# Weight gradients of a SwiGLU FFN: seven Strassen block products in place of eight for four of the five row tiles of dw_gate and dw_up

## The chip, the core and the metric

The kernel runs on one core of one Trainium2 chip. The core has a matrix engine (TensorE, PE in the profile; its weight loads are listed apart as PEld), three engines for elementwise work (VectorE: DVE; ScalarE: ACT; GpSimd: POOL) and SyncE (SP), which here only issues DMAs. Each engine executes its own instructions in order. DMAs are issued from the queues of SP, ACT and POOL and move data between HBM (DRAM), the on-chip memory SBUF and back, some of them transposing on the way. TensorE writes its results to PSUM, which the other engines read. The metric is the device time of one execution in microseconds, and the number compared is the median of several runs.

## The reference

The kernel computes the forward pass and all gradients of a linear-attention block followed by a SwiGLU FFN, in bfloat16, with S = 2048 rows, D = 640 and F = 1728:

```python
def _B_ref(x, w_gate, w_up, w_down):
    g = _silu(x @ w_gate)
    u = x @ w_up
    return (g * u) @ w_down
...
h = x + _A_ref(_layernorm(x, axis=-1), A_wqkv, A_wo)
h2 = h + _B_ref(_layernorm(h, axis=-1), B_w_gate, B_w_up, B_w_down)
...
_out, _vjp = jax.vjp(_f, A_x, A_wqkv, A_wo, B_w_gate, B_w_up, B_w_down)
_grads = _vjp(grad_out)
```

The change is in the gradients of the FFN's weights. With `hn` the normalised `h` (2048 x 640), `m` the product of silu(gate) and up (2048 x 1728), `dh2` the incoming gradient (2048 x 640), and `dg`, `du` the gradients at the outputs of the gate and the up projection (2048 x 1728 each), they are

    dw_gate = hn^T dg      (640 x 1728, out_4)
    dw_up   = hn^T du      (640 x 1728, out_5)
    dw_down = m^T dh2      (1728 x 640, out_6; first computed transposed, as dh2^T m)

## The kernel before

Rows are cut into 16 tiles of 128 (`ST`), the 640 columns of `hn` and `dh2` into 5 tiles of 128 (`DT`). The attention block comes first (up to L607); its last loop writes `h1` (tiles of the pool `work`, stored to DRAM as `scr_h1`) and forms `hn` and its transpose `hnT`. The FFN part (L611 to L731) goes through F in four groups of columns, `GW` = 448, 448, 448 and 384 wide. A group g has two stages:

- **The loop** over eight pairs of row tiles (t = 0, 2, ..., 14). Ten matmuls fill `pg` (L639) and ten `pu` (L644), both halves of one PSUM tile; in group 2 ten more fill `pdm`, while groups 0, 1 and 3 find that product (`dm`) made earlier. ScalarE forms sigmoid(pg) into `dd` (L660), sigmoid(-pg) into `nsg` (L664), and copies `pg` to `m_s` (L665) and `pu` to `u` (L666). VectorE makes `m_s` (m), and in `dd` the `dg` and `du`, by seven elementwise operations (L672). For each row tile SP issues a DMA that transposes its 2w values of `dd` into a `stg` tile (L675, three buffers), and GpSimd issues its store to `scr_dT` (L676). Every second pair GpSimd also stores four row tiles of `m_s` to `scr_m` (L678).
- **The gradient stage.** `dw()` (L702) takes up to two products ("parts"), each a sum over the 16 row tiles, so 16 matmuls into one half of a PSUM tile `ps_dw` (L711). Then one copy takes the tile to a `dwev` tile (L713), and GpSimd issues a store for each part (L715). A `dwd_part(i)` is tile i of dw_down transposed (`dh2` against `m_s`, stored to `scr_dwdT`), a `dgu_part(i, which)` is tile i of dw_gate or dw_up (`hn` against the gate or up half of `dd`, stored to out_4 or out_5). The order is dwd 0 and 1, dgu 0, dgu 1, dwd 2 and 3, dgu 2, dgu 3, dwd 4, dgu 4; dw_down's copies are on VectorE, the others on ScalarE. In all 15 parts, 240 matmuls. The first `dw` puts the row tiles 14 and 15 last (`first=True`), since the loop's elementwise work ends on them.

PSUM is one pool of four tiles of 2 x 512 float32 per partition, taken in turn by `mm(name)`. SBUF is in pools too: `fpool` has six buffers of 2 x 448 bfloat16 per partition that `nsg`, `u`, `a` and `dwev` take in turn (`fw`), and it lies in the area `wB`, opened when the attention block's area `fA` (the tile `rr`) is closed at L609. `work`, with six buffers of 640, is open from start to end; `wk()` takes tiles from it in the attention block and, in the stage after the FFN, in `ln_bwd` (L142), the backward of the layer norm.

`hn` stands as [128, 16, 640]: partition, row tile, column. `dd` is two tiles of eight row tiles each, [128, 8, 896], the gate half and the up half side by side. `m_s` is [128, 16, 448].

The framework's scheduler may reorder an engine's instructions within the limits of their dependencies; in this block (L616) `manual_schedule` fixes SyncE's order as written, and the other engines are left to the scheduler. Waits between engines are put in by the framework from the tiles' uses: a PSUM tile is tracked as a whole, a pool's buffer is handed out again when its last user is done, and so is the area of a closed pool.

After the FFN's last group comes the stage of `ps_dhn` (L109), which takes the transposed `dd` back from `scr_dT` as `cols` tiles. `load_cols(0)` is issued on ScalarE's queue at the start of group 3's gradient stage, `load_cols(1)` in it, behind dwd 4.

Of the kernel before, what the change touches and what calls it, by code (L numbers as in the profile page):

```python
# [20 lines left out]
def kernel(  # L21
# [36 lines left out]
    big = ctx.enter_context(tc.tile_pool(name="big", bufs=5))  # L58
    strips = ctx.enter_context(tc.tile_pool(name="strips", bufs=4))
    small = ctx.enter_context(tc.tile_pool(name="small", bufs=4))  # L60
    work = ctx.enter_context(tc.tile_pool(name="work", bufs=6))

    def mm(name):

# [5 lines left out]
    def half(ap):  # L70
        return ap.rearrange("p (c n) -> p c n", c=2)

    wpools = [work]

    def wk(name, w=D, pool=0):
        return wpools[pool].tile([P, w], BF16, name=name, tag="w", padded_shape=[P, D])
# [98 lines left out]

    fA = ExitStack()
    rr = fA.enter_context(tc.tile_pool(name="fA", bufs=1)).tile([P, 4, 2, D], BF16, name="rr")

    def fw(name):
        return fpool.tile([P, 2, GM], BF16, name=name, tag="f")  # L180
# [430 lines left out]
    fpool = wB.enter_context(tc.tile_pool(name="fpool", bufs=6))  # L611
    zpad = wB.enter_context(tc.tile_pool(name="zpool", bufs=1)).tile([P, 4, 64], BF16, name="zpad")
    nc.gpsimd.memset(zpad[:], 0.0)

    with tc.manual_schedule(engines={EngineType.SP}):
        dh2 = big.tile([P, ST, D], BF16, name="dh2", tag="B")  # L616

        def load_dh2():
# [11 lines left out]
        for g in range(4):  # L630
# [71 lines left out]
            def dw(parts, copy, first=False):  # L702

                ps = mm("ps_dw")
                steps = [(c, t) for c in range(len(parts)) for t in range(ST)]
                if first:

                    steps.sort(key=lambda x: x[1] >= ST - 2)
                for c, t in steps:
                    lhs, rhs, _ = parts[c]  # L710
                    nc.tensor.matmul(ps[:, c, :w], lhsT=lhs(t), rhs=rhs(t), start=(t == 0), stop=(t == ST - 1))  # L711
                ev = fw("dwev")
                last = copy(out=ev[:, :len(parts), :w], in_=ps[:, :len(parts), :w])  # L713
                for c, (_, _, dst) in enumerate(parts):
                    nc.gpsimd.dma_start(out=dst[:, GO[g]:GO[g] + w], in_=ev[:, c, :w])  # L715
                return last
# [6 lines left out]
                        lambda t: dd[t // 8][:, t % 8, which * w:(which + 1) * w],  # L723
                        (out_4, out_5)[which][i * P:(i + 1) * P])

            for i in range(DT):
                if i % 2 == 0:
                    dw([dwd_part(k) for k in range(i, min(i + 2, DT))], nc.vector.tensor_copy, first=(i == 0))
                    if g == 3 and i == 4:
                        load_cols(1, act_load)  # L730
                dw([dgu_part(i, 0), dgu_part(i, 1)], nc.scalar.copy)  # L731

    wB.close()

    M = ctx.enter_context(tc.tile_pool(name="M", bufs=1))
    wpools.append(ctx.enter_context(tc.tile_pool(name="workC", bufs=7)))

    mats = M.tile([P, 3 * DT * D], BF16, name="mats", tag="M")
# [361 lines left out]
```

## Time and the profile before

Three runs took 815.38, 810.91 and 811.22 us: median 811.22. The profiled execution has a span of 809.9 us from the first to the last instruction, 1.3 us under that median, which also takes in what lies around it. The granted TensorE clock is full in every slice.

The stages of the FFN part, from the profile's sums over windows of time (us; the last stage of each group is the gradient stage):

| stage | from | to | length | PE busy | DVE busy | ACT busy | POOL busy |
|---|---|---|---|---|---|---|---|
| all before the FFN | 0 | 141.0 | 141.0 | 139.5 | 123.4 | 73.9 | 49.0 |
| group 0, loop | 141.0 | 172.3 | 31.3 | 31.3 | 28.9 | 25.7 | 10.2 |
| group 0, gradients | 172.3 | 217.7 | 45.4 | 45.4 | 8.4 | 5.3 | 15.7 |
| group 1, loop | 217.7 | 248.1 | 30.4 | 30.4 | 25.5 | 26.0 | 6.6 |
| group 1, gradients | 248.1 | 293.6 | 45.5 | 45.5 | 8.2 | 5.2 | 13.0 |
| group 2, loop (with `pdm`) | 293.6 | 339.0 | 45.4 | 45.4 | 35.8 | 27.6 | 9.8 |
| group 2, gradients | 339.0 | 384.4 | 45.4 | 45.4 | 6.6 | 3.6 | 9.9 |
| group 3, loop | 384.4 | 410.2 | 25.8 | 25.8 | 21.7 | 22.7 | 5.8 |
| group 3, gradients | 410.2 | 449.2 | 39.0 | 39.0 | 7.8 | 4.7 | 18.1 |
| all after the FFN | 449.2 | 809.9 | 360.7 | 357.9 | 207.0 | 90.8 | 68.6 |

How to read it: busy times are sums of the instructions' own spans on an engine; the shape of an instruction is given as partitions x elements with its type, out before in. A row of the groups names line, engine, operation, tiles and count, then busy time and the mean of one in ns, and after the second bar how long the engine was idle just before such instructions and what ended that. In the timeline a row is start, length, engine, line and tiles, and in brackets the wait before it. The DMA table gives, for each kind of transfer, the median from its issue to its landing: `scr_dT` stores from GpSimd's queue 3.2 us at 224 KB and 2.9 at 192 KB, `out_dram` stores from `dwev` 2.1 at 112 KB, `scr_m` stores 4.4 at 448 KB, and `cols` loads on ScalarE's queue 9.8 at 1728 KB.

### The profile page before, as it was taken

To read this page: it belongs to the slowest core of one execution; us is meant where nothing else is said; L and a number is where in the kernel's file an instruction comes from. 1 tells how busy PE (TensorE), PEld (TensorE's weight loads), DVE (VectorE), ACT (ScalarE), POOL (GpSimd) and SP (SyncE) were. 2 spreads that over 40 slices of the span, in tenths; PEclk is the share of its full clock that TensorE was granted. 3 is DMA by queue.
4 is the path that set the end of the run, shared out by engine and by line. 5 is a ranking of instruction groups with operands and counts; after the bars stand their busy time and mean duration, and the time that the engine had idled before them with its cause. 6 is when DMAs were issued, how large, how long until landed. Compare 5 with 4: busy or idle time off the path is not lost.

```text
span 809.9 us, 13757 instructions
## 1 busy us (share of the span) xinstructions
PE 805.5 (99%) x5421; PEld 516.9 (64%) x5421; DVE 473.2 (58%) x883; ACT 285.4 (35%) x398; POOL 206.8 (26%) x369
## 2 busy tenths in 40 slices
PE   9999999999999999999999999999999999999998
PEld 7676566555555555555656677777777777777676
DVE  7989988880095028810850148999897366631212
ACT  6963532750283035400831122322323133322010
POOL 4600047322422312221226301211221121112330
PEclk9999999999999999999999999999999999999999
DMA  9899999997679978991597757977499988999993
GB/s 255 164 246 312 181 244 265 233 259 178 190 168 206 198 189 192 215 252 54 119 242 179 244 149 213 226 195 174 115 208 168 175 154 168 169 239 210 245 214 101
DMA packets 281584, 160.11 MB, mean 198 GB/s; under 512 B 241564, under 2 KB 267293, under 8 KB 281520
## 3 DMA queue, kind: packets, MB, share of 16 engines
q1 hardware_dynamic: 259696, 85.40, 57.8%
q0 software_dynamic: 18928, 68.52, 26.6%
q10 hardware_dynamic: 2896, 5.33, 2.1%
q8 instruction: 42, 0.69, 0.4%
q14 instruction: 22, 0.18, 0.1%
HBM read 47.68 MB, written 53.66 MB: 125 GB/s over the span
## 4 chain that ended last, share of the span: by engine, by line
PE 98%; DVE 1%; DMA 1%; POOL 0%; issue 0%; DVEq 0%
PE ps_dw L711 22%; PE ps_dhn L109 14%; PE ps_dxn L971 8%; PE ps_o L1029 7%; PE pu L644 7%; PE pg L639 7%; PE ps_dwqk L894 5%; PE ps_dm L417 5%; PE ps_kq L305 4%; PE ps_dp L109 3%; PE ps_gt L769 3%; PE ps_y L508 3%; PE ps_dk L109 3%; PE ps_a L571 3%; PE pdm L417 2%; DMA xnT<-xn 1%
## 5 line engine op out<-in xcount | busy, mean ns | idle before, releaser
L109 PE MATMUL ps_dhn<-wgT,cols 128*128 128x320 bf16 x864 | 119.5, 299 | 0.0
L711 PE MATMUL ps_dw<-dd,hn 128*128 128x448 bf16 (+1 forms) x640 | 118.8, 346 | 0.0
L109 PEld LDWEIGHTS <-cols 128*128 128x128 bf16 x864 | 84.4, 98 | 33.0
L711 PEld LDWEIGHTS <-hn 128*128 128x128 bf16 x640 | 62.5, 98 | 54.3
L713 DVE CAST dwev<-ps_dw 128x896 bf16<-128x896 f32 (+3 forms) x12 | 10.9, 907 | 124.6 <-PE ps_dw L711 109.5
L676 POOL DMA_DIRECT2D scr_dT<-stg x64 | 34.7, 542 | 166.2 <-DMA stg<-dd 162.4
L713 ACT CAST dwev<-ps_dw 128x896 bf16<-128x896 f32 (+1 forms) x20 | 17.6, 878 | 160.2 <-PE ps_dw L711 150.8
L147 DVE CUSTOM_DVE_ANT_0 lb_a<-lb_dy,hn 128x640 bf16<-128x640 bf16 x32 | 26.4, 826 | 64.4 <-ACT lb_dy L145 64.4
L644 PE MATMUL pu<-wgu,hnT 128*128 128x448 bf16 (+1 forms) x320 | 63.6, 346 | 0.0
L639 PE MATMUL pg<-wgu,hnT 128*128 128x448 bf16 (+1 forms) x320 | 63.6, 346 | 0.0
L1029 PE MATMUL ps_o<-wd,mT 128*128 128x320 bf16 (+3 forms) x462 | 61.1, 296 | 0.0
L711 PE MATMUL ps_dw<-m_s,dh 128*128 128x448 bf16 (+1 forms) x320 | 60.4, 346 | 0.0
L971 PEld LDWEIGHTS <-ring 128*128 128x128 bf16 x480 | 46.9, 98 | 18.3
L1029 PEld LDWEIGHTS <-mT 128*128 128x128 bf16 (+1 forms) x462 | 41.7, 97 | 17.5 <-issue 2.6
L971 PE MATMUL ps_dxn<-wqkvT,ring 128*128 128x320 bf16 x320 | 51.3, 299 | 0.0
L711 PEld LDWEIGHTS <-dh 128*128 128x128 bf16 x320 | 31.3, 98 | 27.1
L644 PEld LDWEIGHTS <-hnT 128*128 128x128 bf16 x320 | 31.3, 98 | 27.1
L639 PEld LDWEIGHTS <-hnT 128*128 128x128 bf16 x320 | 31.3, 98 | 27.1
L417 PEld LDWEIGHTS <-dh2T 128*128 128x128 bf16 x320 | 31.0, 98 | 25.1
L417 PE MATMUL ps_dm<-wdT,dh2T 128*128 128x448 bf16 (+1 forms) x240 | 46.5, 344 | 0.0
L305 PE MATMUL ps_kq<-wqk,xnT 128*128 128x320 bf16 x320 | 45.0, 300 | 0.4 <-DMA xnT<-xn 0.4
L145 ACT ACTIVATE lb_dy<-ps_dhn,rstd 128x640 bf16<-128x640 f32 x16 | 12.7, 793 | 86.2 <-PE ps_dhn L109 86.2
(168 smaller groups left out, 1306.7 us busy)
## 6 DMA issues: line engine op xcount, KB each, us to landing
scr_dT<-stg POOLq DMA_DIRECT2D x48, 224.0 KB, 3.2
cols<-scr_dT POOLq DMA_DIRECT2D x6, 1728.0 KB, 8.4
scr_m<-m_s POOLq DMA_DIRECT2D x12, 448.0 KB, 4.4
cols<-scr_dT ACTq DMA_DIRECT2D x2, 1728.0 KB, 9.8
out_dram<-dwev POOLq DMA_DIRECT2D x30, 112.0 KB, 2.1
scr_dT<-stg POOLq DMA_DIRECT2D x16, 192.0 KB, 2.9
scr_pq<-pqa SPq DMA_DIRECT2D x4, 640.0 KB, 4.7
scr_xnT<-xnT SPq DMA_DIRECT2D x4, 640.0 KB, 5.3
```

The source lines that it names most:

```text
L109: nc.tensor.matmul(ps[:, ci, :320], lhsT=lhs(k), rhs=rhs(k, *NCH[ci]), start=(start and k == 0), stop=(stop and k == n - 1))
L147: nc.vector.tensor_tensor_reduce(out=a[:], in0=dy[:], in1=xhat, scale=1.0, scalar=0.0, op0=ALU.mult, op1=ALU.add, accum_out=sums[:, 1:2])
L305: nc.tensor.matmul(ps[:, ci, :320], lhsT=xnT[:, t, k, :], rhs=wqk[:, k, w0 + n0:w0 + n1], start=(k == 0), stop=(k == DT - 1))
L417: nc.tensor.matmul(ps[:, c, :w], lhsT=dh2T[:, kt, (t + c) * P:(t + c + 1) * P], rhs=wdT[:, kt, o:o + w], start=(kt == 0), stop=(kt == DT - 1))
L639: nc.tensor.matmul(pg[:, c, :w], lhsT=hnT[:, kt, (t + c) * P:(t + c + 1) * P], rhs=wg[:, kt, 0:w], start=(kt == 0), stop=(kt == DT - 1))
L644: nc.tensor.matmul(pu[:, c, :w], lhsT=hnT[:, kt, (t + c) * P:(t + c + 1) * P], rhs=wg[:, kt, w:2 * w], start=(kt == 0), stop=(kt == DT - 1))
L676: nc.gpsimd.dma_start(out=scr_dT[t + c, :, KO[g]:KO[g] + GK[g], :], in_=stg[:, :GK[g], :])
L711: nc.tensor.matmul(ps[:, c, :w], lhsT=lhs(t), rhs=rhs(t), start=(t == 0), stop=(t == ST - 1))
L713: last = copy(out=ev[:, :len(parts), :w], in_=ps[:, :len(parts), :w])
L894: nc.tensor.matmul(ps[:, ci, :320], lhsT=xn_r[:, t, i * P:(i + 1) * P], rhs=dq[t // 8][:, t % 8, n0:n1] if which == 0 else dk[:, t, n0:n1] ...
L971: nc.tensor.matmul(ps[:, ci, :320], lhsT=lhs[:, i, :], rhs=rhs[:, i, n0:n1], start=(k == 0 and i == 0), stop=(k == 2 and i == DT - 1))
L1029: nc.tensor.matmul(po(t, ci), lhsT=mTs[t // 4][r, t % 4, j, :], rhs=wd[r, j, n0:n1], start=(t, ci) not in opened, stop=last)
```

## The change

For the first four column tiles of `hn`, the two products (gate and up) are computed by Strassen's scheme in Winograd's form, with seven block products in place of eight. `A` stands for the transposed `hn` in 2 x 2 blocks, `B` for `dd` in 2 x 2 blocks: A_mk has the column tiles 2m and 2m+1 and the row tiles of half k (8 of 16), B_kn the row tiles of half k of gate (n = 1) or up (n = 2). Then

    S1 = A21 + A22,  S2 = S1 - A11,  S3 = A11 - A21,  S4 = A12 - S2
    T1 = B12 - B11,  T2 = B22 - T1,  T3 = B22 - B12,  T4 = B21 - T2
    U1 = A11 B11 + A12 B21 = C11            (gate, column tiles 0 and 1)
    U2 = A11 B11 + S2 T2
    U3 = U2 + S3 T3
    C21 = U3 + A22 T4                       (gate, column tiles 2 and 3)
    C22 = U3 + S1 T1                        (up, column tiles 2 and 3)
    C12 = U2 + S1 T1 + S4 B22               (up, column tiles 0 and 1)

Each block product is made for two column tiles (u = 0, 1), each of them 8 matmuls (`prod`, `more`): 7 x 2 x 8 = 112 matmuls where the four column tiles took 4 x 2 x 16 = 128 before. Column tile 4 is done by `dw()` as before, and so is dw_down. A stage has 224 matmuls.

What goes with it:

- The sums S1 to S4 are made on VectorE from `hn`, 8 x 128 = 1024 elements a partition at a time, into tiles of a new pool `sums`; T1, T2 and T3 on VectorE in place of blocks of `dd[0]` and T4 into `m_s`, 8 x 448 (group 3: 8 x 384) elements a partition each.
- Three PSUM tiles are held through the stage: `ps_wa` accumulates A11 B11, then S2 T2, S3 T3 and A22 T4 on top; `ps_wd` takes A12 B21; `ps_wc` S1 T1 and, on top, S4 B22.
- `keep` copies a partial result out of `ps_wa` on ScalarE, in float32, into a `part` tile, which takes one buffer of `fpool`: six in a stage. `evac` adds a kept partial to what stands in PSUM on VectorE and writes the result to `dwev` (C21: a plain copy on ScalarE), a column tile at a time; its stores are on GpSimd's queue as before.
- The order in the stage is written out, and `manual_schedule` now takes in TensorE, VectorE and ScalarE in the FFN's block beside SyncE.
- `load_cols(1)` is issued at the end of group 3's stage.
- `work` is no longer open from start to end: its six buffers lie in `fA` up to the FFN (`workA`), and a new pool `work` is opened when `wB` is closed.

In the built program two things differ outside the gradient stages: the operation that makes `a` stands before the first `nsg` on VectorE in the loops, and the memset of `zpad` stands behind the stores of `h1` on GpSimd.

```diff
@@ -58,7 +58,6 @@
     big = ctx.enter_context(tc.tile_pool(name="big", bufs=5))
     strips = ctx.enter_context(tc.tile_pool(name="strips", bufs=4))
     small = ctx.enter_context(tc.tile_pool(name="small", bufs=4))
-    work = ctx.enter_context(tc.tile_pool(name="work", bufs=6))
 
     def mm(name):
 
@@ -70,7 +69,7 @@
     def half(ap):
         return ap.rearrange("p (c n) -> p c n", c=2)
 
-    wpools = [work]
+    wpools = []
 
     def wk(name, w=D, pool=0):
         return wpools[pool].tile([P, w], BF16, name=name, tag="w", padded_shape=[P, D])
@@ -175,6 +174,7 @@
 
     fA = ExitStack()
     rr = fA.enter_context(tc.tile_pool(name="fA", bufs=1)).tile([P, 4, 2, D], BF16, name="rr")
+    wpools.append(fA.enter_context(tc.tile_pool(name="workA", bufs=6)))
 
     def fw(name):
         return fpool.tile([P, 2, GM], BF16, name=name, tag="f")
@@ -611,8 +611,9 @@
     fpool = wB.enter_context(tc.tile_pool(name="fpool", bufs=6))
     zpad = wB.enter_context(tc.tile_pool(name="zpool", bufs=1)).tile([P, 4, 64], BF16, name="zpad")
     nc.gpsimd.memset(zpad[:], 0.0)
-
-    with tc.manual_schedule(engines={EngineType.SP}):
+    sums = wB.enter_context(tc.tile_pool(name="sums", bufs=1))
+
+    with tc.manual_schedule(engines={EngineType.SP, EngineType.PE, EngineType.DVE, EngineType.Activation}):
         dh2 = big.tile([P, ST, D], BF16, name="dh2", tag="B")
 
         def load_dh2():
@@ -723,16 +724,111 @@
                         lambda t: dd[t // 8][:, t % 8, which * w:(which + 1) * w],
                         (out_4, out_5)[which][i * P:(i + 1) * P])
 
-            for i in range(DT):
-                if i % 2 == 0:
-                    dw([dwd_part(k) for k in range(i, min(i + 2, DT))], nc.vector.tensor_copy, first=(i == 0))
-                    if g == 3 and i == 4:
-                        load_cols(1, act_load)
-                dw([dgu_part(i, 0), dgu_part(i, 1)], nc.scalar.copy)
+            V, A = nc.vector, nc.scalar
+            B11, B12 = dd[0][:, :, 0:w], dd[0][:, :, w:2 * w]
+            B21, B22 = dd[1][:, :, 0:w], dd[1][:, :, w:2 * w]
+
+            def hn_blk(m, k, u):
+                i = 2 * m + u
+                return hn[:, 8 * k:8 * k + 8, i * P:(i + 1) * P]
+
+            def sub(out, in0, in1, op=ALU.subtract):
+                V.tensor_tensor(out=out, in0=in0, in1=in1, op=op)
+
+            def hn_sum(n, u):
+
+                S[n, u] = sums.tile([P, 8, P], BF16, name=f"S{n}", tag=f"S{n}")
+                in0, in1, op = {1: (lambda: hn_blk(1, 0, u), lambda: hn_blk(1, 1, u), ALU.add),
+                                2: (lambda: S[1, u][:], lambda: hn_blk(0, 0, u), ALU.subtract),
+                                3: (lambda: hn_blk(0, 0, u), lambda: hn_blk(1, 0, u), ALU.subtract),
+                                4: (lambda: hn_blk(0, 1, u), lambda: S[2, u][:], ALU.subtract)}[n]
+                sub(S[n, u][:], in0(), in1(), op)
+
+            def prod(ps, u, lhs, rhs, start, stop):
+                for t in range(8):
+                    nc.tensor.matmul(ps[:, u, :w], lhsT=lhs[:, t, :], rhs=rhs[:, t, :],
+                                     start=(start and t == 0), stop=(t == 7), skip_group_check=not start)
+
+            def part32():
+                return fw("part").rearrange("p c n -> p (c n)").bitcast(FP32)[:, :w]
+
+            def out_w(n, m, ev, u0, nu):
+                for u in range(u0, u0 + nu):
+                    i = 2 * m + u
+                    nc.gpsimd.dma_start(out=(out_4, out_5)[n][i * P:(i + 1) * P, GO[g]:GO[g] + w], in_=ev[:, u, :w])
+
+            S, s1, u2, u3 = {}, {}, {}, {}
+            ev = {}
+
+            def evac(n, m, u, in0, in1=None):
+                if (n, m) not in ev:
+                    ev[n, m] = fw("dwev")
+                if in1 is None:
+                    A.copy(out=ev[n, m][:, u, :w], in_=in0)
+                else:
+                    sub(ev[n, m][:, u, :w], in0, in1, ALU.add)
+                out_w(n, m, ev[n, m], u, 1)
+
+            def keep(d, u, ps):
+                d[u] = part32()
+                A.copy(out=d[u], in_=ps[:, u, :w])
+
+            dw([dwd_part(0), dwd_part(1)], V.tensor_copy, first=True)
+            hn_sum(1, 0)
+            dw([dgu_part(4, 0), dgu_part(4, 1)], A.copy)
+            hn_sum(2, 0)
+            hn_sum(3, 0)
+            hn_sum(4, 0)
+            pa, pd, pc = mm("ps_wa"), mm("ps_wd"), mm("ps_wc")
+            for u in range(2):
+                prod(pa, u, hn_blk(0, 0, u), B11, True, False)
+                keep(s1, u, pa)
+            sub(B11, B12, B11)
+            prod(pd, 0, hn_blk(0, 1, 0), B21, True, True)
+            evac(0, 0, 0, pd[:, 0, :w], s1[0])
+            dw([dwd_part(4)], V.tensor_copy)
+            prod(pc, 0, S[1, 0], B11, True, False)
+            hn_sum(1, 1)
+            prod(pd, 1, hn_blk(0, 1, 1), B21, True, True)
+            evac(0, 0, 1, pd[:, 1, :w], s1[1])
+            prod(pc, 1, S[1, 1], B11, True, False)
+            sub(B12, B22, B12)
+            sub(B11, B22, B11)
+            dw([dwd_part(2), dwd_part(3)], V.tensor_copy)
+            T4 = m_s[:, 0:8, :w]
+
+            def more(u, lhs, rhs, last=False):
+                prod(pa, u, lhs, rhs, False, last)
+
+            more(0, S[2, 0], B11)
+            keep(u2, 0, pa)
+            sub(T4, B21, B11)
+            hn_sum(2, 1)
+            more(1, S[2, 1], B11)
+            keep(u2, 1, pa)
+            more(0, S[3, 0], B12)
+            keep(u3, 0, pa)
+            hn_sum(3, 1)
+            evac(1, 1, 0, pc[:, 0, :w], u3[0])
+            more(1, S[3, 1], B12)
+            keep(u3, 1, pa)
+            evac(1, 1, 1, pc[:, 1, :w], u3[1])
+            more(0, hn_blk(1, 1, 0), T4, True)
+            evac(0, 1, 0, pa[:, 0, :w])
+            prod(pc, 0, S[4, 0], B22, False, True)
+            hn_sum(4, 1)
+            evac(1, 0, 0, pc[:, 0, :w], u2[0])
+            more(1, hn_blk(1, 1, 1), T4, True)
+            evac(0, 1, 1, pa[:, 1, :w])
+            prod(pc, 1, S[4, 1], B22, False, True)
+            evac(1, 0, 1, pc[:, 1, :w], u2[1])
+            if g == 3:
+                load_cols(1, act_load)
 
     wB.close()
 
     M = ctx.enter_context(tc.tile_pool(name="M", bufs=1))
+    wpools[0] = ctx.enter_context(tc.tile_pool(name="work", bufs=6))
     wpools.append(ctx.enter_context(tc.tile_pool(name="workC", bufs=7)))
 
     mats = M.tile([P, 3 * DT * D], BF16, name="mats", tag="M")
```

## The prediction

> **What bounds the kernel now.** First the page's busy shares and its chain of waits, for the engine that sets the end:
>
> ```profile
> PE 805.5 (99%) x5421; PEld 516.9 (64%) x5421; DVE 473.2 (58%) x883; ACT 285.4 (35%) x398; POOL 206.8 (26%) x369
> ...
> PE 98%; DVE 1%; DMA 1%; POOL 0%; issue 0%; DVEq 0%
> ```
>
> TensorE runs without a gap, so a matmul taken away is worth its full pace, and a wait put before a matmul costs its full length. The pace stands in the chain in order of time (start, length):
>
> ```profile
> 172.50 45.40 PE ps_dw L711 x240
> ...
> 410.36 39.00 PE ps_dw L711 x240
> ```
>
> 45.40/240 = 0.189 us per 448-column matmul, 39.00/240 = 0.1625 in group 3. Then the rows, by shape, of what the new work resembles:
>
> ```profile
> L672 DVE TENSOR_TENSOR m_s<-m_s,u 128x896 bf16<-128x896 bf16 x24 | 14.8, 619 | 0.0
> ...
> L713 ACT CAST dwev<-ps_dw 128x896 bf16<-128x896 f32 x15 | 13.6, 905 | 123.3 <-PE ps_dw L711 123.3
> ...
> L672 DVE TENSOR_TENSOR m_s<-m_s,u 128x768 bf16<-128x768 bf16 x8 | 4.4, 553 | 0.0
> ...
> L713 ACT CAST dwev<-ps_dw 128x768 bf16<-128x768 f32 x5 | 4.0, 799 | 36.9 <-PE ps_dw L711 27.5 <-DMA out_dram<-dwev 9.4
> ...
> L713 DVE CAST dwev<-ps_dw 128x448 bf16<-128x448 f32 x3 | 1.9, 625 | 43.1 <-PE ps_dw L711 28.1 <-DMA scr_dwdT<-dwev 15.0
> ```
>
> The last two rows show something that costs nothing yet: copies out of PSUM waited 15.0 and 9.4 us for the DMA that empties a `dwev` buffer. The timeline of group 0's and group 3's gradient stages (start, length, engine) shows why:
>
> ```profile
> 201.77 0.54 POOL L676 DMA_DIRECT2D scr_dT<-stg  x1
> ...
> 204.38 0.54 POOL L715 DMA_DIRECT2D scr_dwdT<-dwev  x1
> ...
> 209.89 0.54 POOL L676 DMA_DIRECT2D scr_dT<-stg  x1 [4.96 <-DMA stg<-dd]
> ...
> 210.95 2.13 POOL L715 DMA_DIRECT2D out_dram<-dwev  x4
> ...
> 212.86 0.62 DVE L713 CAST dwev<-ps_dw 128x448 bf16<-128x448 f32 x1 [15.02 <-DMA scr_dwdT<-dwev]
> ```
> ```profile
> 439.62 0.56 POOL L676 DMA_DIRECT2D scr_dT<-stg  x1
> ...
> 441.46 1.08 POOL L715 DMA_DIRECT2D scr_dwdT<-dwev  x2
> ...
> 444.13 2.15 POOL L715 DMA_DIRECT2D out_dram<-dwev  x4
> ```
>
> GpSimd's queue is in order, and the stage's stores stand behind `scr_dT` stores that wait for transposes. The stage of group 0 begins at 172.33, the copy of its first pair ends at 179.7, and that pair is stored at 204 to 210. Group 3 is the same (from 410.2). In groups 1 and 2 the last `scr_dT` store goes out 21.9 and 14.4 us into the stage.
>
> **Matmuls removed.** 144 instead of 160 for w_gate and w_up in a group: 48 x 0.189 + 16 x 0.1625 = 11.7 us, all on the path.
>
> **Waits inside the new stage, stores in time.** The built program names what each matmul waits for. It tracks PSUM by tile, so that a product into one half of `ps_wa` waits for the copy out of the other half (`keep`). One such wait is 0.20 (the `pg` at 164.77 fills its last slot to 166.66, ScalarE starts at 166.86) + 0.53 (905 ns less 448 x 0.83) + 0.05 (a VectorE copy ended at 7.83, the weight load waiting for it began at 7.88) = 0.8 us. It comes three times: between the two first products, and before the third and the fifth of the `more` products. Before the second `more`, VectorE must copy dw23 (1.09), form T4 (3584 elements: 619 + 2688 x 0.516 = 2.0) and S2 (1024: 0.69); with 0.20 ahead, 0.15 behind and 0.09 saved at each of two joints (such operations start 0.53 apart and last 0.62) 3.95 us, of which one product of 1.51 hides: 2.4. Before the fourth, S3 alone: 0.20 + 0.69 + 0.15 = 1.0. The other sums have cover: S1..S4 under the 6.05 us of dgu4, `sub(B11,B12)` under pd and dwd4 (4.5), the two later ones (4.1) under dw23 (6.05); the last S4 with its addition, 1.5, just fits a product. VectorE's three evacuating additions behind them cost 0.62 each and stand before nothing on TensorE. A 448 group stalls 0.8x3 + 2.4 + 1.0 = 5.8, and saves 3.0: +2.8. The 384 group, by the same steps, stalls 5.5 and saves 2.6.
>
> The 1024- and 3584-element operations read hn and dd in pieces of 128 and 448; no row has pieces of 128. The bounds are the bf16 pace above (dd rows in pieces of 448 have it) and 1 ns an element (820 ns for 640 in float32), which adds 2.2 in each of groups 1 to 3 and 0.4 at S3, about 8 in all. I take the former, the dd rows being nearest.
>
> **Waits for buffers.** The six `fpool` buffers now also hold six partial sums. In the built program the copy of dw23 waits for the stores of dw01, and `keep(u2,0)`, before which the second `more` can't start, for those of dgu4. Groups 1 and 2 have landed both by 26 us into the stage; `keep` comes at 32.8. Group 0: its stage is 4.7 later than before (next part), the first product of `more` ends at 172.33 + 4.7 + 168 x 0.189 + 0.8 = 209.6; dgu4's two stores follow the last `scr_dT` of 209.89, the second at 210.95, moved by some 5, and land 2.1 later (the issue table): 218.1; with 0.55 for the copy TensorE resumes at 218.7. Stall 9.1 instead of 2.4. Group 3: the product ends at 410.2 + 168 x 0.1625 + 0.73 = 438.2; dw01's second store, 442.0, lands 2.9 later, then copy, T4 and S2 take 3.2 and the weight load 0.15: 448.25. Stall 10.0 instead of 2.25. Behind the waiting `keep` stand all later copies of ScalarE, behind the copy of dw23 all later sums.
>
> **The start of group 0.** `work` moved into the area that `fpool` takes over. In the built program the first `nsg` therefore waits for the last store of `h1`:
>
> ```profile
> 145.02 0.91 ACT L664 ACTIVATE nsg<-pg 128x896 bf16<-128x896 f32 x1
> 145.32 1.18 POOL L587 DMA_DIRECT2D scr_h<-h  x2
> ...
> 145.82 0.91 ACT L665 CAST m_s<-pg 128x896 bf16<-128x896 f32 x1
> ...
> 146.76 0.62 DVE L672 TENSOR_TENSOR m_s<-m_s,dd 128x896 bf16<-128x896 bf16 x1 [0.93 <-ACT m_s L665]
> ```
>
> The second of those stores starts at 145.95 and lands 4.5 later, 150.4: `nsg` is 5.4 late, and everything behind it on ScalarE and VectorE. VectorE never catches up: its pairs come 3.87 apart (146.76 to 173.87 in seven), TensorE's 3.78. The third `pg` needs the first one's PSUM: 152.25 instead of 149.63, 2.6 of stall; the rest of 5.4 less the 0.86 that m_s of t=14 was early for dw01 (176.76 against slot 28 at 177.62) comes there: together 4.7. dh2's loads, behind `zpad` and the second sigmoid, move by as much as the transposes, hence the 5 above. In each group `a` now stands before the first `nsg` on VectorE and waits for `u`: 0.2, under that margin.
>
> **Moved at no price.** load_cols(1) goes from 444.20 to behind ScalarE's last copy, 1.3 before the stage's end; it lands in 9.8 (both such loads) and is needed 14.7 after the end. It now shares the queues with cols(2): 0 to 3, I take 0. As many stores as before, 15 a group.
>
> **A slower TensorE after a long gap.** Opening matmuls of 128 columns ran 0.11 apart (32 in 3.59 from 1.11), those from 6.99 0.055, though the granted clock says 1.00 for both. The half pace lasted from 1.11 to about 6. After gaps of 9 to 10 us it may return: 0 to 2.5 for each of two, I take 2 each. [...] No gap of this trace is over 1.2 us, so no row here shows it.
>
> **Sum.** Group 0: -3.0 + 4.7 + 12.5 = +14.2; groups 1 and 2: +2.8 each; group 3: -2.6 + 13.2 = +10.6; slow pace after gaps +4. In all +34.4. The profiled span is 809.9, 1.3 under the median of 811.2, which takes in what lies around it: 844.3 and 845.6, so 846.
>
> **Rivals.** (1) The stores land early enough, and the cost is the waits inside the stage alone: 811.2 + 4.7 + 11.3 = 827. For it: medians of 2.1 to 2.9 for landing; against: the 15.0 and 9.4 us waits above. 0.17. (2) TensorE stays at half pace to the stage's end in groups 0 and 3, five products at double: 5 x 1.5 x 2 - 4 = +11, 857. 0.12. (3) VectorE at 1 ns an element: 854. 0.07. (4) Faster: the copies and sums end under the product ahead of them, as all copies of this stage do now without holding TensorE; then only the 11.7 remain, 799.5. It gives a gain of over 1% once stalls sum to under 3.6, 0.9 a group; against it, one `keep` alone is 0.8 and comes three times. 0.04. Forecast: 0.60.
>
> Within 1% (what a measurement here can't tell from no change) means up to 819.3: rival 4 in part and the low end of rival 1, 0.04 together; faster 0.03. The range runs from just above rival 1 to the sum of rivals 2 and half of 3, leaving out 2 in 10: 829 to 862.
>
> **What would show it.** `ps_wa`'s matmuls waiting for ScalarE and for S2, S3; one gap near 9 us in groups 0 and 3, ended by a copy that waited for `dwev` stores; a gap of 2.6 at the third `pg`; 448-column matmuls still 0.189 apart elsewhere. Wrong would be no gaps in group 0 and 3 beyond 3 us, or a stage of group 1 shorter than 45.4.

## The result and the profile after

The changed kernel takes 836.72 us (median of 4 runs, 835.75 to 838.23), the kernel before 811.64 beside it: a ratio of 1.0308, 95% interval 1.0285 to 1.0332. The forecast was 846, with a range of 829 to 862. Ratios in this document leave out executions over 1.5% above the fastest of the same kernel: two of four in e_late, two of twelve in e_best2. The profiled execution has a span of 836.5 us, 26.6 more than that of before. In the page, TensorE is no longer always busy, and a fifth of the chain lies elsewhere:

```profile
PE 801.9 (96%) x5357; PEld 512.1 (61%) x5357; DVE 535.1 (64%) x955; ACT 286.8 (34%) x414; POOL 207.0 (25%) x369
...
PE 81%; DMA 7%; DVE 7%; issue 2%; POOL 2%; ACT 1%; ACTq 0%; POOLq 0%; DVEq 0%; SPq 0%
```

Where it waits is in the view of TensorE's waits from 140 to 481 us (total, times, longest); before the change this stretch has none:

```profile
PE ps_wa L749 <- ACT part L774: 20.6, 12, 9.0
PE ps_wa L749 <- DVE S L736: 6.8, 5, 2.2
PE pg L640 <- ACT m_s L666: 1.8, 1, 1.8
PE ps_dw L712 <- DVE m_s L673: 1.0, 1, 1.0
```

These are 30.2 us. Each of the 19 waits also costs some 0.16, since a matmul that follows another starts 0.189 after it and ends 0.35 after its own start; that makes 3.0. With 4.3 of matmuls at half pace (below) and the 11.7 saved, the sum is 25.8 of the 26.6.

The lengths of the stages, read from the starts of their first matmuls (us):

| | group 0 loop | group 0 gradients | group 1 gradients | group 2 gradients | group 3 gradients |
|---|---|---|---|---|---|
| before | 30.26 | 45.40 | 45.40 | 45.40 | 39.00 |
| after | 32.19 | 57.97 | 48.05 | 48.06 | 49.56 |

Group 1 shows what the stage costs where nothing else is wrong (timeline of TensorE; start, length, then the wait in brackets):

```profile
274.68 1.68 PE L749 MATMUL ps_wa<-dd,hn 128*128 128x448 bf16 x8
276.97 1.67 PE L749 MATMUL ps_wa<-dd,hn 128*128 128x448 bf16 x8 [0.62 <-ACT part L774]
...
293.62 1.68 PE L749 MATMUL ps_wa<-dd,S 128*128 128x448 bf16 x8
297.50 1.69 PE L749 MATMUL ps_wa<-dd,S 128*128 128x448 bf16 x8 [2.21 <-DVE S L736]
299.81 1.67 PE L749 MATMUL ps_wa<-dd,S 128*128 128x448 bf16 x8 [0.62 <-ACT part L774]
302.27 1.69 PE L749 MATMUL ps_wa<-dd,S 128*128 128x448 bf16 x8 [0.79 <-DVE S L736]
304.57 1.67 PE L749 MATMUL ps_wa<-m_s,hn 128*128 128x448 bf16 x8 [0.62 <-ACT part L774]
```

Five waits, each in front of a product into `ps_wa`. In group 0 the second is not 2.21 but 9.03, and the timeline of all engines shows the chain behind it:

```profile
206.82 1.68 PE L749 MATMUL ps_wa<-dd,S 128*128 128x448 bf16 x8
207.19 1.07 POOL L716 DMA_DIRECT2D scr_dwdT<-dwev  x2
208.31 0.54 POOL L677 DMA_DIRECT2D scr_dT<-stg  x1
210.63 1.09 DVE L714 CAST dwev<-ps_dw 128x896 bf16<-128x896 f32 x1 [6.62 <-DMA scr_dwdT<-dwev]
...
213.63 0.54 POOL L677 DMA_DIRECT2D scr_dT<-stg  x1 [4.78 <-DMA stg<-dd]
214.16 1.07 POOL L716 DMA_DIRECT2D out_dram<-dwev  x2
...
216.94 0.53 ACT L774 COPY part<-ps_wa 128x448 f32<-128x448 f32 x1 [24.48 <-DMA out_dram<-dwev]
217.52 3.15 PE L749 MATMUL ps_wa<-dd,S 128*128 128x448 bf16 x8 [9.03 <-ACT part L774]
```

GpSimd waits 4.78 for a transpose, then stores dgu4, which ScalarE had copied at 188.08, 25 us earlier; only then has ScalarE a buffer for the partial sum, and TensorE goes on. Its next eight matmuls take 3.15 us in place of 1.68.

### The profile page after: what moved, and what is told of

It is laid out like the page before. It is cut to its first block, busy times and chain, and to the rows that moved or that the text cites. A ratio compares the mean times of both kernels' runs of the same rounds, so it can differ in the third digit from the quotient of the medians.

```text
span 836.5 us, 13751 instructions
## 1 busy us (share of the span) xinstructions
PE 801.9 (96%) x5357; PEld 512.1 (61%) x5357; DVE 535.1 (64%) x955; ACT 286.8 (34%) x414; POOL 207.0 (25%) x369
## 4 chain that ended last, share of the span: by engine, by line
PE 81%; DMA 7%; DVE 7%; issue 2%; POOL 2%; ACT 1%; ACTq 0%; POOLq 0%; DVEq 0%; SPq 0%
PE ps_dhn L108 14%; PE ps_dxn L1067 8%; PE ps_o L1125 7%; PE ps_dw L712 6%; PE ps_wa L749 5%; PE ps_dwqk L990 5%; PE ps_dm L417 5%; PE pg L640 4%; PE pu L645 4%; PE ps_kq L305 3%; DMA stg<-dd 3%; PE ps_a L571 3%; PE ps_dk L108 3%; PE ps_dp L108 3%; PE ps_gt L865 3%; PE ps_y L508 3%
## 5 line engine op out<-in xcount | busy, mean ns | idle before, releaser
L749 PEld LDWEIGHTS <-S 128*128 128x128 bf16 x256 | 25.6, 102 | 49.7 <-DVE S L736 21.1
L749 PE MATMUL ps_wa<-dd,S 128*128 128x448 bf16 (+1 forms) x128 | 29.8, 382 | 23.1 <-ACT part L774 16.4
L774 ACT COPY part<-ps_wa 128x448 f32<-128x448 f32 (+1 forms) x24 | 12.4, 519 | 115.1 <-PE ps_wa L749 70.0
L1132 DVE TENSOR_TENSOR h1r<-ps_o,h1r 128x640 bf16<-128x640 f32 x15 | 12.1, 823 | 52.6 <-PE ps_o L1125 45.4
```

Of the source, the lines that this page charges most:

```text
L749: nc.tensor.matmul(ps[:, u, :w], lhsT=lhs[:, t, :], rhs=rhs[:, t, :], start=(start and t == 0), stop=(t == 7), skip_group_check=not start)
```

## The experiments

**e_plain: the seven products undone, all else of the change kept.**

```diff
-            dw([dwd_part(0), dwd_part(1)], V.tensor_copy, first=True)
...
-            evac(1, 0, 1, pc[:, 1, :w], u2[1])
+            for i in range(DT):
+                if i % 2 == 0:
+                    dw([dwd_part(k) for k in range(i, min(i + 2, DT))], nc.vector.tensor_copy, first=(i == 0))
+                dw([dgu_part(i, 0), dgu_part(i, 1)], nc.scalar.copy)
```

> The changed kernel with the seven products undone: its gradient stage makes the fifteen sums of 16 row tiles with 240 matmuls in the old order, and everything else of the change stays (pools, written-out order of TensorE, VectorE and ScalarE, load_cols(1) at the stage's end). Theory (what the change costs comes from the waits inside the new stage, but for the first nsg): 811.6 + 1.9 for the gap at the third pg + up to 1.1 at the stage's start, 813 to 815, with stages of 45.4 in groups 1 and 2. Rival (the written-out order or the moved pools cost something by themselves that the gaps do not show): 818 or more.

815.08 us, ratio 1.0044 (1.0021 to 1.0068): at the upper end of the theory's 813 to 815. The stages are 46.85, 45.40, 45.40 and 39.00 us, group 0 is 3.0 longer in all, and TensorE's waits in the stretch are the first `nsg`'s alone:

```profile
PE pg L640 <- ACT m_s L666: 1.4, 1, 1.4
PE ps_dw L712 <- DVE m_s L673: 1.1, 2, 1.0
```

So the written-out order costs nothing that a gap doesn't show, the late first `nsg` some 3 us, and the other 22 belong to the new stage.

**e_pools: the pools laid out so that `nsg` takes over no buffer of `h1`.**

```diff
-    rr = fA.enter_context(tc.tile_pool(name="fA", bufs=1)).tile([P, 4, 2, D], BF16, name="rr")
     wpools.append(fA.enter_context(tc.tile_pool(name="workA", bufs=6)))
+    rr = fA.enter_context(tc.tile_pool(name="fA", bufs=1)).tile([P, 4, 2, D], BF16, name="rr")
...
+    sums = wB.enter_context(tc.tile_pool(name="sums", bufs=1))
     fpool = wB.enter_context(tc.tile_pool(name="fpool", bufs=6))
-    sums = wB.enter_context(tc.tile_pool(name="sums", bufs=1))
```

> The changed kernel with its pools laid out in another order and nothing else: the tiles of h1 lie at the head of the area, then rr; after the area is closed the tiles of the sums come first and fpool last, so that the first nsg takes no buffer over from h1. Theory (the changed kernel's first nsg waits 4.67 us for a store of h1, and TensorE pays for it with gaps of 1.77 at the third pg and 0.97 in dw01): both gaps go, and with some 0.16 for each restart that is 3.1; group 0's transposes start earlier by about as much, so the 9.03 us gap keeps its length or shrinks by 1. 832.5 to 833.7, against 836.7. Rival (VectorE, whose pairs come 3.87 apart against TensorE's 3.78, sets the start of the stage anyway): only the 1.77 goes or moves into the gap of dw01, 834.9 to 836.7.

837.76 us, 1.0318 (1.0288 to 1.0348): no gain, which neither theory had. Both early gaps are gone, and group 0's loop takes 30.27 again. But the long gap grew to 10.15, and in groups 1 and 2 the matmuls behind the 2.21 us wait ran slow. TensorE's timeline in group 1, and the sums by windows there (window, its length, busy time and count of PE, PEld, DVE, ACT, POOL, then the granted clock, DMA share, GB/s):

```profile
292.44 1.68 PE L749 MATMUL ps_wa<-dd,S 128*128 128x448 bf16 x8
296.32 3.13 PE L749 MATMUL ps_wa<-dd,S 128*128 128x448 bf16 x8 [2.21 <-DVE S L736]
```
```profile
292.00:296.30 4.30, 2.12 (x12) 0.88 (x9) 3.63 (x3) 0.53 (x1) 1.07 (x2) 1.00 1.25 235
296.30:299.50 3.20, 3.13 (x8) 1.18 (x9) 0.00 (x0) 0.01 (x1) 0.00 (x0) 0.52 0.38 111
```

The granted clock is 0.52 in the 3.2 us behind the gap. It cost 1.45 us there and 1.3 in group 2, and some 0.8 more in group 0. So the wait for the store is shown and its price was really paid, but this run can't show its worth in the time: it is of the size of what the clock adds or leaves out.

**e_pd: another product between the first two.**

```diff
-            for u in range(2):
-                prod(pa, u, hn_blk(0, 0, u), B11, True, False)
-                keep(s1, u, pa)
+            prod(pa, 0, hn_blk(0, 0, 0), B11, True, False)
+            keep(s1, 0, pa)
+            prod(pd, 0, hn_blk(0, 1, 0), B21, True, True)
+            prod(pa, 1, hn_blk(0, 0, 1), B11, True, False)
+            keep(s1, 1, pa)
             sub(B11, B12, B11)
-            prod(pd, 0, hn_blk(0, 1, 0), B21, True, True)
             evac(0, 0, 0, pd[:, 0, :w], s1[0])
```

> The changed kernel with one product moved in every group: A12 B21 of column tile 0 goes into ps_wd between the two A11 B11 products into ps_wa, in place of after them. Theory (the gap of 0.62 before the second A11 B11 product is the copy of ps_wa's other half, since PSUM is tracked by tile, and any other product of 1.51 covers it): this gap is gone in all four groups, four times 0.62 + 0.16 = 3.1, 833 to 834. Rival (the gap belongs to the copy's place on ScalarE behind the copy of dgu4, and moves with it): the gap stays, or turns up before the next product that reads T1, 836 to 837.5.

The 0.62 us gap is gone in all four groups and not before the next product that reads T1, as the theory had it: it is the copy out of the other half of the PSUM tile, and another product covers it. The time, 835.53 us (832.04 to 838.16), 1.0282 (1.0247 to 1.0318), is less clear, and the theory's price of 3.1 was too high. In group 3 the saving came up again in the wait for buffers, which ends with a store and not with TensorE's own work (6.20 in place of 5.47; in group 0 the store came earlier too, 7.75 in place of 9.03), and in the profile half pace took back 1.3 us in group 1.

**e_ladder: T4 formed twice in group 1 and three times in group 2.**

```diff
-            sub(T4, B21, B11)
+            for _ in range(1 + (0, 1, 2, 0)[g]):
+                sub(T4, B21, B11)
```

> The changed kernel with T4 formed twice in group 1 and three times in group 2 (the same values again), which lengthens VectorE's work ahead of the second S2 product by 1.95 and 3.9 us. Theory: the gaps of 2.21 there grow to 4.2 and 6.1, each microsecond of it paid in full, 5.85 in all; and the matmuls after the longer ones run slower as they do after the 9.03 gap (eight in 3.15 us in place of 1.68), so somewhere between 2.2 and 9 us of idleness there is a point from which a gap costs some 1.5 more: 842.5 to 845.5. Rival (the slow matmuls of groups 0 and 3 have to do with the DMA traffic there, not with the idle time before them): eight matmuls take 1.68 after both gaps, 842.5.

848.84 us in a single run, above the range of both. The gaps are 4.26 and 6.33, as expected, and the matmuls behind both run at half pace (in group 1 eight in 3.17 us, at a granted clock of 0.50); the rival, DMA traffic, is out. The price was too small: the second eight are slow too (2.24 in group 1 in place of 1.67, 1.93 in group 2). That is 0.8 of the 3.3 us above the range, and group 3's wait, 6.46 in place of 5.47, is 1.0 more; the rest stays open with one run.

```profile
298.01 3.17 PE L749 MATMUL ps_wa<-dd,S 128*128 128x448 bf16 x8 [4.26 <-DVE S L736]
301.80 2.24 PE L749 MATMUL ps_wa<-dd,S 128*128 128x448 bf16 x8 [0.62 <-ACT part L774]
```

**e_stores: the first stores of a stage on ScalarE's queue.**

```diff
-            def dw(parts, copy, first=False):
+            def dw(parts, copy, first=False, q=nc.scalar):
...
-                    nc.gpsimd.dma_start(out=dst[:, GO[g]:GO[g] + w], in_=ev[:, c, :w])
+                    q.dma_start(out=dst[:, GO[g]:GO[g] + w], in_=ev[:, c, :w])
...
-                    nc.gpsimd.dma_start(out=(out_4, out_5)[n][i * P:(i + 1) * P, GO[g]:GO[g] + w], in_=ev[:, u, :w])
+                    (nc.scalar if (n, m) == (0, 0) else nc.gpsimd).dma_start(out=(out_4, out_5)[n][i * P:(i + 1) * P, GO[g]:GO[g] + w], in_=ev[:, u, :w])
```

> The changed kernel with the stores of dw_down's tiles, of column tile 4 and of C11 issued from ScalarE's queue in place of GpSimd's, in the same places of the program. Theory (the gaps of 9.03 in group 0 and 5.47 in group 3 are waits for fpool buffers whose stores stand on GpSimd's queue behind scr_dT stores): the gap of group 0 falls to the 2.2 of groups 1 and 2 and that of group 3 to under 1, the slow matmuls after them (3.15 and 2.72 us for eight) go back to 1.68 and 1.46, and the time falls by 6.8 + 1.6 + 4.7 + 2 = 15, to 820 to 824. Rival (the stores are late because the DMA engines are full of transposes, whichever queue issues them): the two gaps stay above 4 us and the time above 831.

872.24 us, 1.0721 (1.0688 to 1.0755): far worse than either expectation. The 9.03 us gap did fall to 2.21, but in each group a new one of 8 to 14 us stands before the second A11 B11 product. ScalarE's timeline in group 1 shows it (ACTq is ScalarE's sequencer issuing a DMA):

```profile
276.72 5.33 ACTq L716 DMA_DIRECT2D scr_dwdT<-dwev  x2
282.08 0.91 ACT L714 CAST dwev<-ps_dw 128x896 bf16<-128x896 f32 x1 [11.10 <-DMA stg<-dd]
292.07 1.75 ACTq L716 DMA_DIRECT2D out_dram<-dwev  x2
293.85 0.53 ACT L774 COPY part<-ps_wa 128x448 f32<-128x448 f32 x1 [10.86 <-issue]
```

The copy of dgu4 (at 282.08) stood behind dw01's two stores, and its row names a transpose of `dd` (`DMA stg<-dd`) as the end of its 11.10 us of waiting. The store of dgu4 went out 9 us after this copy had ended, and `keep` stood behind it. The row of `keep` names nothing for its 10.86 us of waiting; that the store waited for a transpose too, as on GpSimd's queue, is the author's estimate from the first of the two waits. The rival (full DMA engines) isn't tested by this run, but the changed kernel's trace speaks against it: the stores that the two gaps waited for landed 2.2 us (dgu4's in group 0, issued at 214.69) and 1.9 us (dw01's in group 3, issued at 460.14) after they were issued, no more than the medians of such stores, 2.2 and 1.9. They were late in being issued.

**e_late: GpSimd's order written out, stores ahead of the last transposes.**

```diff
-    with tc.manual_schedule(engines={EngineType.SP, EngineType.PE, EngineType.DVE, EngineType.Activation}):
+    with tc.manual_schedule(engines={EngineType.SP, EngineType.PE, EngineType.DVE, EngineType.Activation, EngineType.Pool}):
...
-                for c in range(2):
-                    stg = stage()
...
+                def tail(t):
+                    for c in range(2):
+                        stg = stage()
...
+                if t < 10 or g in (1, 2):
+                    tail(t)
+
+            def late(*ts):
+                if g in (0, 3):
+                    for t in ts:
+                        tail(t)
...
             dw([dgu_part(4, 0), dgu_part(4, 1)], A.copy)
+            late(10)
...
             dw([dwd_part(4)], V.tensor_copy)
+            late(12)
...
             evac(0, 0, 1, pd[:, 1, :w], s1[1])
+            late(14)
+            if g == 0:
+                load_wdT(wdT, 2)
```

> The changed kernel with GpSimd's order written out too, and in groups 0 and 3 the transposes and scr_dT stores of row tiles 10 to 15 put behind the stores of dw01 and dgu4 (10, 11), of dwd4 (12, 13) and of C11 (14, 15); the same stores on the same queue. Theory (the gaps of 9.03 and 5.47 are waits for buffers whose stores stand behind scr_dT stores): group 0's gap falls to about 2.2 and group 3's under 1.5, and the slow matmuls behind them become fewer: 819 to 825. Rival (the stores land late because the DMA engines are full, as the stores on ScalarE's queue did): a gap over 5 us stays in group 0, 830 or more.

A ratio of 1.0137 (1.0084 to 1.019), that is some 823 us, in the expected range; but the four runs spread from 821.77 to 840.21, and the profile is of the longest, so it doesn't show what the shorter ones gained. The edit also moves the transposed load of w_down (`load_wdT`) behind row tile 15. In the profile the wait in group 0 is 2.21, but a new one came: with GpSimd's order written out, the loads of `dh2` stand behind the first `scr_dT` stores, and dw01 waits for them.

**e_late2: the same, with those loads first.**

```diff
                     wait_for(sig, load_dh2())
+                    tail(0)
                     load_wgu(1)
...
+                if (g > 0 or t > 0) and (t < 10 or g in (1, 2)):
+                    tail(t)
```

> e_late with dh2's four loads put ahead of the first scr_dT stores on GpSimd's queue, where the changed kernel has them; in e_late they stood behind, and dw01 waited for them four times. Nothing else differs. Theory (stores behind scr_dT stores make the gaps of 9.03 and 5.47): the waits for dh2 go, group 0's gap is 2.2, group 3's under 3, no eight matmuls take over 3 us behind them, and the time is 819 to 825. Rival (moving the stores up pushes the transposes and the loads back by as much): 830 or more, with a wait for dh2 or for cols in the rows of TensorE.

831.2 us (823.18 to 833.55), 1.0225 (1.0187 to 1.0262): over the expected range and in the rival's, though not with the rival's waits for dh2 or cols. Group 0 did what the theory said: its long gap is 2.21, nothing is slow behind it, and the stage takes 49.49 in place of 57.97. Group 3 did not. TensorE there:

```profile
453.60 2.07 PE L761 MATMUL ps_wa<-dd,S 128*128 128x384 bf16 x8 [3.10 <-DVE S L748]
...
470.06 2.72 PE L761 MATMUL ps_wa<-m_s,hn 128*128 128x384 bf16 x8 [5.36 <-ACT dwev L779]
```

The 5.47 us wait has turned into 3.10 and, behind four more products, 5.36, for a copy whose buffer was to come from the stores of dw23; these went out only at 466.68, behind `scr_dT` stores and behind loads of the next stage, one of which waited 2.45 itself. In group 0 the place of the stores is thereby shown to be the cause of the gap. In group 3 this run moved the waits and didn't remove them; there it is shown by the runs below, where e_order, with the stores at their old places, keeps a wait of 6.26 and e_best3, with them moved, has none. Moving only some of the stores ahead helps where the rest have time.

**e_order: another order of the same 224 matmuls.**

```diff
+            run(p4, 0, g4[0])
...
+            prod(pa, 0, hn_blk(0, 0, 0), B11, True, False)
+            keep(s1, 0, pa)
...
+            prod(pd, 0, hn_blk(0, 1, 0), B21, True, True)
...
+            prod(pa, 1, hn_blk(0, 0, 1), B11, True, False)
...
+            more(0, S[2, 0], B11)
+            keep(u2, 0, pa)
...
+            run(p23, 0, d23[0])
+            more(1, S[2, 1], B11)
+            keep(u2, 1, pa)
+            run(p23, 1, d23[1])
...
+            more(0, S[3, 0], B12)
...
+            run(p5, 0, dwd_part(4))
...
+            more(1, S[3, 1], B12)
```

> The changed kernel with another order of the same 224 matmuls in a stage, so that a product of another PSUM tile, or a dw_down tile, stands between any two that touch ps_wa and behind every operand that VectorE has to form; S tiles take turns in the same four buffers, T2 is formed in two halves. Pools and store queues as in the changed kernel. Theory: in groups 1 and 2 no gap is left and a stage is 224 x 0.189 = 42.4 us (5.7 under the 48.05 of the changed kernel); in groups 0 and 3 the waits for fpool buffers stay, since two more are asked for before the stores land: 817 to 828. Rival (VectorE, with some 20 us of sums in a stage, is late somewhere else as soon as the waits are moved): gaps of over 1 us in groups 1 and 2, 829 or more.

824.62 us (823.77 to 827.17), 1.0154 (1.0118 to 1.019): in the range. Groups 1 and 2 take 43.82 and 43.81 us, not the 42.4 of the theory. One gap is left in each, of 1.28 before the first S4 product, where an addition still read the other half of `ps_wc`. Groups 0 and 3 keep waits of 2 to 6 us, for buffers in the main.

**e_best, e_best2, e_best3: order, pools and stores together.** Each mends what the profile of the one before showed.

> That other order together with the pools laid out as in e_pools and the store order of e_late. Theory: every wait that the changed kernel added is covered or gone, and what remains is the gain of 64 matmuls, 11.7 us: 799.5 to 804, under the 811.6 of before. Rival (something else takes the place of the gaps: the stores that are moved up hold back the transposes, or the next group's first operations wait for fpool buffers): 808 or more.

821.78 us, 1.012 (1.007 to 1.017): the rival's range, not the theory's. Group 1's `keep(u2,1)` waited for dw01's stores, and group 0's dw01 for `dh2`:

```profile
290.76 3.15 PE L759 MATMUL ps_wa<-dd,S 128*128 128x448 bf16 x8 [6.24 <-ACT part L784]
```

> e_best with what its profile showed mended: dh2's loads ahead of the scr_dT stores; the stores of dw01, dgu4 and C11 ahead of scr_dT stores 10 to 15 in all four groups (with the loads and transposes that SyncE issues after a loop behind them), since keep(u2,1) waited 6.24 us in group 1 for dw01's; dwd4 cut into two runs of eight matmuls, so that one stands behind each of the two S3 products (the first S4 product waited 1.28 us in each group for an addition that read ps_wc); T4 formed in place of T2, so that load_cols(1) can go out before the stage's end. Theory: nothing is left in the stages but their 224 matmuls: 800 to 804, under the 811.6 of before. Rival (each wait that is covered uncovers the next, stores or transposes above all): 808 or more.

815.79 us (808.89 to 822.12), 1.0026 (0.9996 to 1.0056): the rival's range again. The gradient stages of groups 0 to 2 are without a gap, but the later transposes held back the load of w_gate, and in group 3 ScalarE's queue waited 17.18 us at `load_cols(1)`:

```profile
292.23 3.63 PE L652 MATMUL pg<-wgu,hnT 128*128 128x448 bf16 x10 [5.28 <-DMA wgu<-in_B_w_gate_dram]
...
457.90 2.72 PE L768 MATMUL ps_wa<-dd,hn 128*128 128x384 bf16 x8 [9.33 <-ACT dwev L786]
```

The last puts the stores of rows 10 to 15 at places of their own in each group, and `load_cols(1)` back at the end:

```diff
+        LATE = [("g4", "ev", "p23"), ("dw", "ev0", "g4"), ("dw", "ev0", "g4"), ("g4", "ev", "p23")]
...
+            def late(at):
+                for t, point in zip((10, 12, 14), LATE[g]):
+                    if point == at:
+                        tail(t)
...
+            run(p5, 0, dwd_part(4), range(8))
             more(1, S[3, 1], B12)
             keep(u3, 1, pa)
+            run(p5, 0, dwd_part(4), range(8, ST))
```

> e_best2 with the two places mended that its profile showed, where group 2's first pg waited 5.28 us for w_gate and group 3 waited 9.33 us for a copy that stood on ScalarE's queue behind load_cols(1): in groups 1 and 2 the scr_dT stores of row tiles 10 to 15 go out earlier (behind the stores of dw01, of C11's first tile and of dgu4), so that the transposes of the weights and the loads behind them start sooner; load_cols(1) and the stores of the last 64 columns of m_s and of zpad go back to where the changed kernel has them. Theory: no gap over 1 us in any of the four stages and none between them, 224 matmuls a stage: 800 to 804, under the 811.6 of before. Rival (a wait that these edits move comes up at another place, as it did three times): 808 or more.

802.95 us (799.61 to 811.55), 0.991 (0.9877 to 0.9943): lower than the kernel before by 0.9%, with the interval clear of 1, and than the changed kernel by some 34 us. Four of its eight runs lie in the expected 800 to 804 or just under it, and what the longer ones waited for no profile shows. The page of a run of 801.42 and its waits of TensorE from 140 to 481 us:

```profile
PE 793.3 (99%) x5357; PEld 510.4 (64%) x5357; DVE 537.3 (67%) x959; ACT 287.8 (36%) x414; POOL 206.9 (26%) x369
```
```profile
PE ps_wc L772 <- DVE dd L759: 1.1, 1, 1.1
PE ps_wa L772 <- ACT dwev L790: 0.6, 1, 0.6
```

The stages take 44.39, 42.38, 42.38 and 36.40 us: 224 x 0.189 = 42.3 and 224 x 0.1625 = 36.4, the bare matmuls, but for 2.0 in group 0. VectorE is as busy as in the changed kernel (537.3 against 535.1), so the amount of its sums was not the bound; where they stood was.

## Why the prediction was right, and where it wasn't

**The direction and its mechanism were right.** Matmuls were worth their full pace, and waits before matmuls cost their full length. e_plain leaves 3.4 of the 25 us, and e_best3, with the same 224 matmuls and the waits gone, gives 9.0 of the 11.7 us saved (10.2 in the profiled execution).

**The waits inside a stage** (forecast 5.8 in a 448 group, +2.8 net) were 0.62 three times, 2.21 and 0.79, each with 0.16 more, 5.65 in all; the stages of groups 1 and 2 are 2.65 longer. e_pd shows that such a wait is the other half's copy. VectorE took 0.69 for 1024 elements in pieces of 128 and 2.02 for 3584 in pieces of 448: the faster of the two prices, so rival 3 is out.

**The wait for buffers in group 0** (forecast 9.1, TensorE resuming at 218.7) was 9.03, at 217.52. That the length fits so well is in part luck: both its ends came 1.1 to 1.2 earlier than forecast, because the group began less late (next paragraph). e_late2 brings it to 2.21. Rival 1, stores in time, is out, and so is rival 2: from the third product behind the gaps on, the pace is 1.69 and 1.47 for eight.

**The start of group 0** was mis-sized: forecast 4.7, measured 1.9 in the loop and 1.1 at the stage's start. The store landed at 149.87 and not 150.4, so the third `pg` waited 1.77 and not 2.6; and of the lateness that the forecast carried on to dw01 only 0.97 and its restart arrived, less than the 2.1 put down. That VectorE doesn't catch up before dw01 held; how far it is behind when dw01 needs it was overstated.

**Group 3** is the term that was furthest off: +12.6 forecast with its 2 for the slow pace, 49.56 - 39.00 = 10.56 measured, of which 28 matmuls of `ps_dhn` are work of the next stage done early:

```profile
456.80 1.46 PE L749 MATMUL ps_wa<-dd,S 128*128 128x384 bf16 x8
458.10 2.06 PE L108 MATMUL ps_dhn<-wgT,cols 128*128 128x320 bf16 x14
465.64 2.72 PE L749 MATMUL ps_wa<-dd,S 128*128 128x384 bf16 x8 [5.47 <-ACT part L774]
468.15 1.27 PE L108 MATMUL ps_dhn<-wgT,cols 128*128 128x320 bf16 x4
469.22 2.29 PE L749 MATMUL ps_wa<-dd,S 128*128 128x384 bf16 x8
```

At 29.5/216 = 0.137 each they are 3.8 us, and the net price is 6.7. The order of the built program has them between the `more` products; the forecast priced the gap as if TensorE had nothing else to do in it. The rest is the store: issued at 460.14 and landed in 1.9 (forecast 461.9 and 2.9), so that TensorE resumed 2.5 earlier than forecast.

**The slow pace after gaps** (2 each, 4 in all) was 1.47 + 0.19 in group 0 and 2.65 in group 3 (1.26 and 0.83 on two products, 0.56 on four `ps_dhn`): 4.3. Right in the sum, by luck in the parts, which are under and over the 2. What the forecast did not have is that a gap of 2.2 can bring it on too (last section). The granted clock of 1.00 that it read for the slow opening is no measurement: the trace's record of the clock begins at 6.35 us.

The forecast of 846 was 9.3 too high: 5.9 of it from group 3, 1.7 from group 0 (its start, as above), 0.3 from groups 1 and 2, 0.4 from rounding up, and 1.1 because the profiled execution was one of the longer ones (its span is 0.2 under the median, in before 1.3).

## What to carry to other kernels

When an engine that is never idle is relieved of work, count how many new joints the new form puts before its instructions: here 16 matmuls were saved in a stage and five joints added, and the joints cost twice the saving until other work was laid into each. Before a pool is asked for buffers for new purposes, look at when its old buffers are really emptied: a copy that waited 15 us at no price told that the stores were late, and the new user stood on the path. Where a stall is priced, look in the built order for what the engine has queued behind it and for what else stands in the queues it is moved to.

## What the runs showed of the hardware

Behind some of the gaps TensorE ran at half pace, and the granted clock was low there. Here are windows of the changed kernel, cut where a gap begins or ends and where the clock changes, group 0 first, then group 3 (after the length come busy time and count of PE, PEld, DVE, ACT, POOL; the granted clock is third from the end):

```profile
206.82:208.49 1.67, 1.67 (x9) 0.69 (x7) 0.00 (x0) 0.00 (x0) 1.62 (x4) 1.00 0.44 175
208.49:211.48 2.99, 0.00 (x1) 0.00 (x0) 0.85 (x1) 0.00 (x0) 0.36 (x1) 1.00 1.07 177
211.48:217.52 6.04, 0.00 (x0) 0.10 (x1) 2.78 (x3) 0.53 (x1) 3.89 (x8) 0.50 0.81 235
217.52:221.72 4.20, 3.58 (x10) 1.38 (x10) 0.00 (x0) 0.53 (x1) 0.36 (x1) 0.50 0.22 82
221.72:224.30 2.58, 1.79 (x10) 0.74 (x9) 1.10 (x2) 0.53 (x1) 0.00 (x0) 1.00 0.04 10
```
```profile
460.17:464.07 3.90, 0.00 (x0) 0.00 (x0) 1.93 (x2) 0.00 (x0) 3.90 (x8) 1.00 0.63 210
464.07:465.64 1.57, 0.00 (x1) 0.10 (x2) 1.29 (x2) 0.48 (x1) 1.57 (x4) 0.50 0.55 186
465.64:470.89 5.25, 5.25 (x18) 2.53 (x18) 0.00 (x0) 0.48 (x1) 0.36 (x1) 0.50 0.15 54
470.89:474.00 3.11, 3.11 (x21) 1.84 (x20) 1.16 (x2) 0.67 (x2) 0.54 (x1) 1.00 0.00 0
```

The clock fell 3.0 us into the gap of 9.03 and came back 4.2 us after the matmuls began; in the gap of 5.47 it fell after 3.9 and came back 5.25 after they began. From 221.72 to 464.06, over the gaps of 2.21 in groups 1 and 2, it was 1.00. In e_pools it was 0.52 in the 3.2 us behind such a gap (above). What eight matmuls took behind the longer gaps of six profiles, 448 columns wide (1.67 to 1.69 us at full pace):

| run, group | gap (us) | the eight behind it (us) |
|---|---|---|
| e_pools, 0 | 10.15 | 3.17 |
| changed kernel, 0 | 9.03 | 3.15 |
| e_pd, 0 | 7.75 | 3.14 |
| e_ladder, 1 | 4.26 | 3.17 |
| e_order, 0 | 2.94 | 1.67 |
| e_order, 0 | 2.58 | 2.22 |
| changed kernel, 1 and 2 | 2.21 | 1.69, 1.69 |
| e_pools, 1 and 2 | 2.21 | 3.13, 2.47 |
| e_pd, 1 and 2 | 2.21 | 2.40, 1.69 |
| e_late2, 0, 1 and 2 | 2.21 | 1.69, 1.69, 1.69 |
| e_order, 0 | 2.16 | 1.67 |

In group 3, with 384 columns, eight took 2.72 in place of 1.46 behind the gap of 5.47 and behind that of 5.36 in e_late2, 6.26 in e_order and 9.33 in e_best2, and 2.07 behind that of 3.10 in e_late2. Behind the wait of 1.77 at the third `pg` of the changed kernel ten matmuls took 2.05, as without a wait (2.05 and 2.06). So of the nine gaps of 2.21 three were followed by slow matmuls, 1.3 to 1.45 us each with the eight after them, and six were not; 2.94 cost nothing of this kind in e_order. The length of a gap alone doesn't decide it, and what does isn't shown here.
